# Sixteen block sums made ahead of the second attention's token product, and the copies of the keys' products dealt out anew

## The chip, the cores and the metric

The kernel runs on one core of a Trainium2 chip. The core has a matrix engine (TensorE, "PE" in the profile), a vector engine (VectorE, "DVE"), a scalar engine (ScalarE, "ACT"), a general engine (GpSimd, "POOL") and a queue that issues the loads and stores (SyncE, "SP"). The metric is the device time of one execution in microseconds, the median of several. Three executions of the kernel before took 1470.37, 1470.67 and 1471.87 us.

## The reference

Four layers work on a sequence of 2048 tokens of width 1024: linear attention, a gated feed-forward layer, and both once more with the same weights. Each layer takes the normalised input and adds its result to the input. The linear attention is, cut to its core:

```python
q, k, v = split(layernorm(x) @ wqkv)          # 32 heads of width 32
phi = lambda t: where(t > 0, t + 1, exp(t)) + 1e-6
pq, pk = phi(q), phi(k)
kv  = einsum("bhsd,bhse->bhde", pk, v)        # sums over all tokens
z   = einsum("bhsd->bhd", pk)
out = x + (einsum(pq, kv) / (einsum(pq, z) + 1e-6)) @ wo
```

## The kernel before

The 2048 tokens are 16 tiles of 128; four tiles make a quarter. The kernel never forms `v`. It forms the **token product** M, the transposed normalised input times `pk` summed over all tokens, and multiplies that by the weights of `v` afterwards. The stage is the function `m_products`.

**Seven products instead of eight.** Many of the large products use Strassen's scheme in Winograd's form: a product of two-by-two blocks takes seven block products, for which sums and differences of blocks have to be made first on VectorE. In `m_products` the token axis is halved, so tile `i` (0 to 7) goes with tile `NS + i` (8 to 15), and the width is halved into columns 0 to 511 and 512 to 1023. For each `i` eight sums are made, four of the normalised input (`n1` to `n4`) and four of the keys (`k1` to `k4`), all through `op` (L514); together 64, each of 128 by 512 two-byte elements. They depend on one another: `n2` needs `n1`, and `n4` needs `n2`, the keys likewise. `n1`, `n2`, `k1` and `k2` write into the memory of `x[8+i]`, whose contents have by then been sent away to DRAM; the others overwrite halves of their own inputs.

**The order in `m_products`.** TensorE goes through seven products of 32 matmuls each, and after every eight matmuls calls `later.tick()`. `later` holds tasks by due tick. The 64 sums are handed out four to a tick, in the order (`n1`,`k1`), (`n2`,`k2`), (`n3`,`k3`), `n4`, `k4`:

```python
jobs = [(f, i) for fs in ((n1, k1), (n2, k2), (n3, k3), (n4,), (k4,))
        for i in range(NS) for f in fs]
for n, (f, i) in enumerate(jobs):
    later.at(1 + n // 4, lambda f=f, i=i: self.behind(last_k, f, (i,)))
```

so they take ticks 1 to 16. `behind` queues them after the last key's last instruction. The first two products need no sums; the third reads `n1` and `k1`, the fourth `n2` and `k2`, the fifth `n4`, the sixth `n3` and `k3`, the seventh `k4`. The third product's result is copied by ScalarE (`keep`), and after each quarter of the fourth product VectorE adds that copy to the fourth's result (`add`, L556); the fifth product accumulates onto these sums. Here VectorE and GpSimd run in the order written (`manual_schedule`); elsewhere the compiler's planner orders each engine's instructions by program order and its own estimate of when each can start.

**The denominators** run beside it, from tick 10 on: `z_mult` (GpSimd, L690) multiplies a query tile by the keys' sums, `z_sum` two ticks later (VectorE, L695 to L697) sums by head, adds the small constant and inverts, `z_scale` two ticks later (GpSimd, L702) scales the tile, and `q_turn` (SP, L711) transposes it by DMA. `z_chain` starts the next tile two or three ticks after the last. All use one buffer, `ksum`, so the product of a tile waits for the reduction of the tile before it.

**The second attention ahead of it** (`l == 2`). Eight units of the first quarter's keys are run (`first`, eight ticks). Then `todo`, a hand-made list of 24 units, alternates keys of the second quarter with the queries of quarters 0 and 1, which `blocks("q", 0)` makes by the seven-product scheme in four steps (`one` to `four`) for each of four token tiles `j`; one unit of the third quarter's queries is put in as well. The other seven of these follow, and `blocks("k", 2)` makes the keys of quarters 2 and 3, the tiles `j` in pairs. Each result goes through `phi`: ScalarE's relu (L407) and exp (L408), then VectorE's join (L411). In `one`, two PSUM results are copied: the first product's onto bank `Y`, and the fifth's (`v`) to SBUF. For queries ScalarE makes both; for keys VectorE copies `Y` for odd `j` and `v` for every `j` (L635), ScalarE the rest (L637). `v` has bank `kv0` for every `j` of the keys, so a `v` waits for the copy of the one before it. Each key tile is also added into `ksum` on GpSimd (L482).

**After `m_products`** come the third quarter's remaining queries and `fold_wo` (L726), which needs the output weights `o0`. Their load is issued on SP while the seventh product runs, in SP's order behind transposed query tiles.

Of the kernel before, what the change touches and what calls it, by code (L numbers as in the profile page):

```python
# [10 lines left out]
F32 = mybir.dt.float32  # L11
# [3 lines left out]
P = 128  # L15
NW = 512
HD = 32
QT = 4
# [74 lines left out]
class _Net:  # L93
# [345 lines left out]
    def layer_A(self, l, last_ln):  # L439
# [5 lines left out]
        kv = []  # L445
# [79 lines left out]
        def m_products(q_first):  # L525

            NS = self.NS
            copy = lambda out, src: nc.scalar.activation(out=out, in_=src, func=ACT.Copy)
            X = [self.ps.tile([P, NW], F32, tag="a", name=f"mx{j}") for j in range(QT)]
            Y = [self.ps3.tile([P, NW], F32, tag="b", name=f"my{j}") for j in range(2)]  # L530
            Y += [self.kvp.tile([P, NW], F32, tag=f"kv{j}", name=f"my{2 + j}") for j in range(2)]
            mt, V, M5 = [], [], []
            last_k = self.last_phi
            jobs = [(f, i) for fs in ((n1, k1), (n2, k2), (n3, k3), (n4,), (k4,))
                    for i in range(NS) for f in fs]
            for n, (f, i) in enumerate(jobs):
                later.at(1 + n // 4, lambda f=f, i=i: self.behind(last_k, f, (i,)))

            def product(A, B, banks, start, done):
                for j in range(QT):  # L540
                    for i in range(NS):
                        nc.tensor.matmul(banks[j], lhsT=A(i)[:, j * P:(j + 1) * P], rhs=B(i),  # L542
                                         start=start and i == 0, stop=i == NS - 1,
                                         skip_group_check=True)
                    done(j)
                    later.tick()

            def evict(banks, h, n):
                return lambda j: copy(half(mt[h][:, j, :], n), banks[j])

            def keep(j):
                M5.append(self.temp(name="m5"))
                copy(M5[j], V[j])

            def add(out, j):
                nc.vector.tensor_tensor(out=out, in0=Y[j], in1=M5[j], op=ALU.add)  # L556

            product(lambda i: half(xn(i), 0), lambda i: half(pk(i), 0), X, True,
                    lambda j: copy(Y[j], X[j]))
            mt += [self.slot(f"mt{l}_{h}", [P, 4, D]) for h in range(2)]  # L560
            product(lambda i: half(xn(NS + i), 0), lambda i: half(pk(NS + i), 0), X, False,
                    evict(X, 0, 0))
            z_row()
            later.at(2 if l else 6, lambda: z_chain(0))
            V += [self.ps.tile([P, NW], F32, tag="a", name=f"mv{j}") for j in range(QT)]
            product(lambda i: part(i, 0), lambda i: part(i, 2), V, True, keep)
            product(lambda i: part(i, 1), lambda i: part(i, 3), Y, False, lambda j: add(V[j], j))
            product(lambda i: f16(half(xn(NS + i), 0)), lambda i: half(pk(NS + i), 1), V, False,
                    evict(V, 0, 1))
            product(lambda i: f16(half(xn(i), 1)), lambda i: f16(half(pk(i), 1)), Y, False,  # L570
                    lambda j: add(half(mt[1][:, j, :], 1), j))
            kv.extend(self.ps.tile([P, NW], F32, tag="a", name=f"kv{l}_{i}") for i in range(H))

            def steps(h, b):
                for j in range(QT):
                    kv_half(h * QT + j, mt[h][:, j, :], b)

            def last(j):
                copy(half(mt[1][:, j, :], 0), Y[j])
                if j < 3:  # L580
                    steps(*((0, 1), (1, 1), (0, 0))[j])
                if j == 1:
                    ring.load_to(ring.index((l, "o0")) + 1)

            product(lambda i: half(xn(NS + i), 1), lambda i: f16(half(pk(NS + i), 0)), Y, False, last)
            q_first()
            later.tick()
            steps(1, 0)
            ring.load_to(ring.index((l, "o1")) + 1)
            finish_kv()  # L590
# [19 lines left out]
        def blocks(p, first):  # L610


            xa, xb = self.xnT[l, first], self.xnT[l, first + 1]
            s1, s2, s3, s4 = self.xs[l, first // 2]
            r0, r1, t0, t1 = (ring.get((l, n)) for n in (f"{p}0", f"{p}1", f"t{p}0", f"t{p}1"))
            t0, t1 = (t[:, :, :].bitcast(F16) for t in (t0, t1))
            A = {1: xa[:, 0:4], 2: xa[:, 4:8], 3: s4, 4: xb[:, 4:8], 5: s1, 6: s2, 7: s3}
            B = {1: r0[:, 0:4], 2: r0[:, 4:8], 3: r1[:, 4:8], 4: t1[:, 0:4], 5: t0[:, 0:4],
                 6: t1[:, 4:8], 7: t0[:, 4:8]}
            if p == "q":  # L620
                for sc in range(first, first + 2):
                    a = self.slot(f"pq{l}_{sc}", [P, QT, D])
                    for i in range(QT):
                        pq_of[sc, i] = a[:, i, :]

            def put(src, q, j, n):
                t = (first + q) * QT + j
                cols = slice(n * NW, (n + 1) * NW)
                self.phi(src, (pq_of[first + q, j] if p == "q" else self.pk_home(l, t))[:, cols])
                if p == "k":  # L630
                    later.at(1, lambda: k_sum(t, cols))

            def copy(out, src, vector):
                if vector:
                    nc.vector.tensor_copy(out=out, in_=src)  # L635
                else:
                    nc.scalar.activation(out=out, in_=src, func=ACT.Copy)  # L637

            def steps(j):
                S = {}  # L640

                def mm(m, bank, start=False):
                    for k in range(4):
                        nc.tensor.matmul(by_row(bank), lhsT=A[m][:, k, j * P:(j + 1) * P],  # L644
                                         rhs=B[m][:, k, :].rearrange("p (b i d) -> p i b d", i=R, d=HD),
                                         start=start and k == 0, stop=k == 3, skip_group_check=True)

                def one():
                    S["X"] = self.ps.tile([P, NW], F32, tag="a", name=f"qx{j}")
                    mm(1, S["X"], True)  # L650
                    if p == "k" and j == 2:
                        S["Y"] = self.kvp.tile([P, NW], F32, tag="kv1", name=f"qy{j}")
                    else:
                        S["Y"] = self.ps3.tile([P, NW], F32, tag="b", name=f"qy{j}")
                    copy(S["Y"], S["X"], p == "k" and j % 2)
                    v = self.kvp.tile([P, NW], F32, tag=f"kv{j % 2 if p == 'q' else 0}", name=f"qv{j}")
                    mm(5, v, True)
                    S["V"] = self.temp(name="qm5")
                    copy(S["V"], v, p == "k")

                def two():
                    mm(2, S["X"])
                    put(S["X"], 0, j, 0)
                    mm(6, S["Y"])
                    S["Z"] = self.ps.tile([P, NW], F32, tag="a", name=f"qz{j}")
                    nc.vector.tensor_tensor(out=S["Z"], in0=S["Y"], in1=S["V"], op=ALU.add)

                def three():
                    mm(7, S["Y"])
                    nc.vector.tensor_tensor(out=S["V"], in0=S["Y"], in1=S["V"], op=ALU.add)  # L670
                    put(S["V"], 1, j, 1)
                    mm(3, S["Z"])
                    put(S["Z"], 0, j, 1)

                def four():
                    mm(4, S["Y"])
                    put(S["Y"], 1, j, 0)

                return one, two, three, four

            return [steps(j) for j in range(QT)]
# [144 lines left out]
        def run(*lists):  # L826

            n = max(len(u) for u in lists)
            for i in range(n):
                for u in lists:  # L830
                    if i < len(u):
                        u[i]()
                        later.tick()

        if l == 0:
            steps = self.head()
        else:
            ring.load_to(ring.index((l, "tq1")) + 1)
            for j in range(QT):
                later.at(1 + j, lambda j=j: self.sums_x(l, 0, j))  # L840
# [19 lines left out]
        else:  # L860
# [4 lines left out]
            for j in range(QT):  # L865
                todo += [next(k), Q[j][1], next(k), Q[j][2]] + ([Q[j + 1][0]] if j + 1 < QT else []) + [Q[j][3]]
            q2 = row_major(q_unit, 2)
            run(todo[:-1] + q2[:1] + todo[-1:])
            later.at(1, lambda: ring.load_to(ring.index((l, "tk1")) + 1))
            self.xs[l, 1] = [self.x[self.NS + i][:, :].bitcast(F16).rearrange("p (a n) -> p a n", n=NW)  # L870
# [433 lines left out]
```

## Time and profile before

| engine | busy of 1468.3 us | instructions |
|---|---|---|
| TensorE matmul | 1456.5 (99%) | 6927 |
| VectorE | 872.9 (59%) | 1546 |
| ScalarE | 577.5 (39%) | 1037 |
| GpSimd | 287.1 (20%) | 190 |

The second attention spans about 736 to 945 us of the profile. Its stages can be told apart by the lines of TensorE's instructions: L465 and L644 are projections, L542 the token product, L498 the product with the weights of `v`, L726 the fold, L738 the output.

| stage | from, us | to, us |
|---|---|---|
| first quarter's keys | 736.4 | 750.0 |
| `todo` and the third quarter's queries | 750.0 | 801.8 |
| keys of quarters 2 and 3 | 801.8 | 827.3 |
| token product | 827.3 | 885.8 |
| remaining queries, fold, output | 885.8 | 944.9 |

In the views, a row of the waits gives who waited for whom, the total in us, how often, and the longest. A row of the chain gives the start, the length, and the engine, tile and line. A row of the timeline also names output, inputs and shape, and in brackets the idle time before it.

### The profile page before, as it was taken

The numbers are of one execution on the slowest core, as the hardware profiler recorded it, in microseconds if no ns is written. First come the engines' busy times: TensorE is split into PE (matmuls) and PEld (weight loads), VectorE is DVE, ScalarE is ACT, GpSimd is POOL, SyncE is SP. The second block draws the span as 40 slices with busy tenths as digits, with TensorE's granted clock in tenths as the row PEclk, the third lists the DMA queues.
The fourth block names the chain that finished last, engine by engine and source line by source line (L and its number), as shares of the span: only waits on it lengthen the run. The fifth ranks groups of instructions, "written<-read, shape, count | busy, mean of one in ns | idle before, by whom it ended". The sixth has DMA issues, their size and how long they took to land.

```text
span 1468.3 us, 18717 instructions
## 1 busy us (share of the span) xinstructions
PE 1456.5 (99%) x6927; PEld 660.3 (45%) x6927; DVE 872.9 (59%) x1546; ACT 577.5 (39%) x1037; POOL 287.1 (20%) x190
## 2 busy tenths in 40 slices
PE   9999999999999999999999989999999999999999
PEld 4444444444444444444444434444444444444444
DVE  7978698666684654455476886766445434433632
ACT  6772574333340333340078616633333203333200
POOL 1354851011100011110031577410110001111000
PEclk9999999999999999999999999999999999999999
DMA  9940787564559996445933119965444687444461
GB/s 283 236 155 10 184 217 205 186 219 165 202 169 259 342 300 216 143 143 187 297 97 87 58 29 259 274 228 186 144 143 151 180 260 249 147 147 148 149 204 43
DMA packets 323883, 268.09 MB, mean 183 GB/s; under 512 B 106064, under 2 KB 295888, under 8 KB 321872
## 3 DMA queue, kind: packets, MB, share of 16 engines
q1 hardware_dynamic: 312784, 245.60, 56.7%
q10 hardware_dynamic: 11008, 21.30, 3.9%
q8 instruction: 54, 0.88, 0.2%
q14 instruction: 37, 0.30, 0.1%
HBM read 203.42 MB, written 38.80 MB: 165 GB/s over the span
## 4 chain that ended last, share of the span: by engine, by line
PE 93%; DVE 3%; DMA 1%; ACT 1%; POOL 1%; issue 0%; SPq 0%; DVEq 0%; ACTq 0%; POOLq 0%
PE ps L465 11%; PE dy L1150 10%; PE yu L1051 10%; PE yg L1051 10%; PE dx L1150 7%; PE dv L1150 7%; PE xg L1051 6%; PE xu L1051 6%; PE ps L738 4%; PE zg L1051 3%; PE zu L1051 3%; PE vu L1051 3%; PE vg L1051 3%; PE my L542 2%; PE mx L542 2%; PE qy L644 1%
## 5 line engine op out<-in xcount | busy, mean ns | idle before, releaser
L1051 PEld LDWEIGHTS <-w 128*128 128x128 f16 (+1 forms) x3136 | 306.7, 98 | 371.9 <-issue 2.5
L1104 POOL TENSOR_TENSOR h<-m5u,m5g 128x512 f16<-128x512 f32 x56 | 72.0, 1285 | 810.6 <-DVE m5u L1100 760.2
L465 PE MATMUL ps<-w,xnT 128*128 128x512 bf16 x768 | 170.1, 379 | 0.5 <-DMA w<-in_A_wqkv_dram 0.3
L1150 PEld LDWEIGHTS <-h 128*128 128x128 f16 x1120 | 109.6, 98 | 132.2
L1087 DVE TENSOR_TENSOR zg<-yg,m5g 128x512 f32<-128x512 f32 x56 | 39.2, 699 | 188.5 <-PE yg L1051 185.1
L1051 PE MATMUL yg<-s,w 128*128 128x512 f16 x448 | 115.0, 379 | 0.1
L465 PEld LDWEIGHTS <-xnT 128*128 128x128 bf16 x768 | 74.3, 98 | 90.5 <-issue 1.7
L1051 PE MATMUL yu<-s,w 128*128 128x512 f16 x448 | 115.0, 379 | 0.0
L1051 PE MATMUL xg<-xnT,w 128*128 128x512 f16 x448 | 115.0, 379 | 0.0
L1051 PE MATMUL xu<-xnT,w 128*128 128x512 f16 x448 | 115.0, 379 | 0.0
L1059 ACT ACTIVATE m5g<-m5g 128x512 f32<-128x512 f32 x56 | 35.2, 629 | 174.8 <-DVE m5g L1100 174.8
L1150 PE MATMUL dy<-w,h 128*128 128x512 f16 x448 | 98.0, 379 | 0.0
L1150 PE MATMUL dx<-w,h 128*128 128x512 bf16 x448 | 97.3, 379 | 0.0
L408 ACT ACTIVATE e<-e,eps 128x512 f32<-128x512 f32 x128 | 91.0, 720 | 3.3
L690 POOL TENSOR_TENSOR kvc<-pq,kvc 128x1024 f32<-128x1024 bf16 x32 | 78.5, 2452 | 60.1 <-DVE den L695 39.7
L738 PE MATMUL ps<-T,pqT 128*128 128x512 bf16 x384 | 83.6, 379 | 0.0
L1068 ACT ACTIVATE m5g<-vg 128x512 f32<-128x512 f32 x56 | 33.4, 597 | 110.9 <-PE vg L1051 85.2
L482 POOL TENSOR_TENSOR kvc<-kvc,slab 128x512 f32<-128x512 f32 x46 | 56.8, 1240 | 79.9 <-DVE slab L411 79.3
L1062 DVE TENSOR_TENSOR h<-yu,r 128x512 f16<-128x512 f32 x56 | 38.7, 691 | 56.0 <-PE yu L1051 56.0
L407 ACT ACTIVATE e<-ps 128x512 f32<-128x512 f32 x96 | 56.6, 590 | 34.1 <-PE ps L465 33.6
L1100 DVE TENSOR_TENSOR m5u<-yu,m5u 128x512 f32<-128x512 f32 x56 | 38.7, 691 | 49.4 <-PE yu L1051 48.4
L1150 PEld LDWEIGHTS <-e 128*128 128x128 f16 x448 | 43.8, 98 | 52.8
(191 smaller groups left out, 2108.4 us busy)
## 6 DMA issues: line engine op xcount, KB each, us to landing
w<-in_B_W_gate_dram SPq DMA_DIRECT2D x56, 512.0 KB, 5.7
w<-in_B_W_up_dram SPq DMA_DIRECT2D x56, 512.0 KB, 5.3
w<-td SPq DMA_DIRECT2D x32, 896.0 KB, 4.7
w<-in_B_W_down_dram SPq DMA_DIRECT2D x24, 896.0 KB, 5.3
w<-tg SPq DMA_DIRECT2D x42, 512.0 KB, 6.9
w<-tu SPq DMA_DIRECT2D x42, 512.0 KB, 6.5
w<-in_A_wqkv_dram SPq DMA_DIRECT2D x9, 1024.0 KB, 7.5
away<-x SPq DMA_DIRECT2D x16, 512.0 KB, 4.5
```

Of the source, the lines that this page charges most:

```text
L407: nc.scalar.activation(out=e, in_=ps, func=ACT.Relu, scale=-1.0)
L408: nc.scalar.activation(out=e, in_=e, func=ACT.Exp, scale=-1.0, bias=self.eps6[:, 0:1])
L465: nc.tensor.matmul(by_row(ps), lhsT=self.xnT[l, l_q][:, kt, j * P:(j + 1) * P], rhs=w[:, kt, :].rearrange("p (b i d) -> p i b d", i=R, d=H ...
L482: nc.gpsimd.tensor_tensor(out=ksum[:, cols], in0=ksum[:, cols], in1=pk, op=ALU.add)
L542: nc.tensor.matmul(banks[j], lhsT=A(i)[:, j * P:(j + 1) * P], rhs=B(i), start=start and i == 0, stop=i == NS - 1, skip_group_check=True)
L690: nc.gpsimd.tensor_tensor(out=prod, in0=pq_of[sc, j], in1=zrow, op=ALU.mult)
L738: nc.tensor.matmul(ps, lhsT=pqT[sc][:, g, j * P:(j + 1) * P], rhs=T[g // 4][:, g % 4, n2 * NW:(n2 + 1) * NW], start=(g == 0), stop=(g == G ...
L1051: nc.tensor.matmul(ps, lhsT=W[w][m][:, k, :], rhs=A[m][:, k, :], start=start and k == 0, stop=k == 3, skip_group_check=True)
L1062: self.last_put = nc.vector.tensor_tensor(out=h[:, b, :], in0=ps, in1=R.pop(b), op=ALU.mult)
L1087: self.last_z = nc.vector.tensor_tensor(out=Z[w], in0=Y[w], in1=V[w], op=ALU.add)
L1104: nc.gpsimd.tensor_tensor(out=h[:, 3, :], in0=V["u"], in1=V["g"], op=ALU.mult)
L1150: nc.tensor.matmul(banks[j], lhsT=A(k)[:, j * P:(j + 1) * P], rhs=w[:, i, :], start=start and k == 0, stop=k == self.U - 1, skip_group_che ...
```

## The change

Two things are changed, both in the second attention alone.

**The sums.** For `i` = 4 to 7, the sums `n1`, `n2`, `n3` and `k1` are made while the queries run, four to a batch, at ticks 16, 19, 22 and 25 after the first eight units; each batch is queued behind the join that was the last one then. `m_products` leaves these 16 out of its list and hands out the other 48, still four to a tick. The aim is to take work from VectorE in the token product and give it to a stretch where VectorE has room.

**The copies.** For the keys' seven-product tiles, the copies of `Y` for `j` = 0 and of `v` for `j` = 0 are ScalarE's, all others VectorE's. `Y` of tile 2 thus moves from ScalarE to VectorE, and `v` of tile 0 from VectorE to ScalarE. `v` of tile 1 goes to bank `kv1`, so that it no longer waits for the copy of tile 0's.

```diff
+            made = made_early
             jobs = [(f, i) for fs in ((n1, k1), (n2, k2), (n3, k3), (n4,), (k4,))
-                    for i in range(NS) for f in fs]
+                    for i in range(NS) for f in fs if (f, i) not in made]
...
-                    copy(S["Y"], S["X"], p == "k" and j % 2)
-                    v = self.kvp.tile([P, NW], F32, tag=f"kv{j % 2 if p == 'q' else 0}", name=f"qv{j}")
+                    copy(S["Y"], S["X"], p == "k" and j)
+                    v = self.kvp.tile([P, NW], F32, tag=f"kv{j % 2 if p == 'q' or j < 2 else 0}", name=f"qv{j}")
                     mm(5, v, True)
                     S["V"] = self.temp(name="qm5")
-                    copy(S["V"], v, p == "k")
+                    copy(S["V"], v, p == "k" and j)
...
+        made_early = set()
+
+        def make_early(ticks, *fs):
+
+            for tick, i in ticks:
+                for f in fs:
+                    made_early.add((f, i))
+                later.at(tick, lambda i=i: [self.behind(self.last_phi, f, (i,)) for f in fs])
...
             q2 = row_major(q_unit, 2)
+            make_early([(16 + 3 * j, QT + j) for j in range(QT)], n1, n2, n3, k1)
             run(todo[:-1] + q2[:1] + todo[-1:])
```

## The prediction

> **What bounds the kernel now.** I first read the busy times and the slices: TensorE is busy for 99% of the span at nearly full clock, so a change to VectorE's work pays only where TensorE waits. The waits of TensorE over the second attention (745 to 945 us) show where that is:
>
> ```profile
> PE mv L542 <- DVE slab L514: 2.7, 3, 1.7
> PE mv L542 <- DVE mv L556: 1.8, 1, 1.8
> PE qv L644 <- DVE qm L635: 0.9, 1, 0.9
> PE fold L726 <- DMA w<-in_A_wo_dram: 0.8, 1, 0.8
> ```
>
> The columns are total, times, longest. Four waits, 6.2 us. The upper two lie in the fifth block product (bank `mv`): for sums `n4` (tile `slab`, L514) and for the additions of L556. The third lies in the keys, for a copy that the change deals out anew; the fourth is the fold's wait for `o0`. The query stretch shows no wait of TensorE.
>
> Waits alone understate the fifth product. The windows have, after the times: length, then busy time of PE, PEld, DVE, ACT, POOL, then clock, DMA share, GB/s:
>
> ```profile
> 749.90:801.80 51.90, 51.90 (x243) 23.50 (x240) 32.33 (x56) 44.05 (x75) 12.72 (x11) 1.00 0.24 62
> 855.40:869.30 13.90, 9.46 (x33) 3.55 (x33) 13.83 (x23) 1.79 (x3) 6.47 (x4) 0.88 0.20 40
> 859.60:863.40 3.80, 3.76 (x10) 1.41 (x11) 3.73 (x8) 0.60 (x1) 1.60 (x1) 0.55 0.20 39
> ```
>
> The fifth product takes 13.9 us. Its 32 matmuls need 32 x 0.216 = 6.9 us (64 of the same shape take 13.83 us in the chain, 0.216 each). So 7.0 us are lost, with VectorE busy 13.8 of 13.9. The third row shows that part of it isn't idleness: for 3.8 us the clock was 0.55.
>
> Why VectorE is late is in the chain:
>
> ```profile
> 843.03 9.18 POOL kvc L690
> ...
> 852.23 1.23 DVE den L695
> ...
> 853.98 0.66 DVE mv L556
> 854.64 4.01 DVE slab L514 x4
> 858.65 0.61 DVE mv L556
> 859.26 1.33 DVE slab L514 x4
> 860.59 1.14 DVE den L695
> ...
> 862.24 0.67 DVE mv L556
> 862.91 4.01 DVE slab L514 x4
> 866.92 0.62 DVE mv L556
> ```
>
> This is VectorE's written order: ticks 1 to 12 hold 48 sums, then comes the first denominator, then the four additions with the last 16 sums (`n4`, `k4`) between them. VectorE ends its 48 sums at about 850.1, then stands 2.0 us, because the denominator waits for GpSimd's product:
>
> ```profile
> 843.03 9.17 POOL L690 TENSOR_TENSOR kvc<-pq,kvc 128x1024 f32<-128x1024 bf16 x1 [8.19 <-ACT kvc L492]
> 853.53 2.12 POOL L690 TENSOR_TENSOR kvc<-pq,kvc 128x1024 f32<-128x1024 bf16 x1 [1.33 <-DVE den L695]
> ```
>
> The same instruction takes 9.17 us while sums stream and 2.12 us otherwise. Conversely, four sums begun after GpSimd's took 4.01 us, against 1.33 us undisturbed.
>
> [...]
>
> **The change part by part.**
>
> *Token product.* The list shrinks from 64 to 48: `n1`,`k1` 8, `n2`,`k2` 12, `n3`,`k3` 12, `n4` 8, `k4` 8. At four a tick they end with tick 12, where in order of issue they still precede the first denominator. So the stream before it stays at 48 sums, ending at about 850.1: I give the first three 0.82 + 1.30 + 1.29 us as now (they collide with GpSimd's key sums), the other 45 0.336 each. GpSimd's first product stays locked out until then, and the first denominator still ends at 853.97. But no sums are left between the additions. The first is then done at 854.64, before the fifth product starts at 855.4. The second follows at 855.3 (needed 857.1). Then comes the second denominator: GpSimd's product ends at 855.65, so it runs to 857.45, and the third addition ends at 858.1 (needed 858.8), the fourth at 858.7 (needed 860.6). `n4` runs at about 844 to 847; it overwrites what the second product reads until 841.1, so it needn't wait. All 7.0 us go, slow clock included, the tightest margin being 0.7 us. **-7.0.**
>
> *Does the denominator chain hold the stages after it?* It now runs at GpSimd's pace, one product and one scaling in 2.07 + 1.88 = 3.95 us. The sixth scaling, behind which SP issues `o0`, ended at 885.93; it should end at 857.7 + 5 x 3.95 = 877.5. So it comes forward by more than TensorE does.
>
> *Fold.* `o0` was issued at 887.29, 1.4 us after that scaling, and landed 5.5 us later; now it lands at about 884.4. TensorE reaches the fold at 892.0 - 7.0 = 885.0. `finish_kv`'s scaling on VectorE (L594, now ending at 892.1) moves with TensorE and costs some 0.2. I take 0.6 of the 0.8 us. **-0.6**, between -0.8 and 0.
>
> *Keys.* Moving tile 0's `v` copy to ScalarE and tile 1's `v` to `kv1` removes a wait of 0.1 us at 805.84. ScalarE stood idle for 1.62 us there, which hides its new copy. For tile 3, `v` still waits in `kv0` for tile 2's copy, and VectorE now has tile 2's `Y` copy to make beside it. It was held by a join to 816.5, made another to 817.1 and the copy to 817.7; with one more 0.6 us copy in front, the 0.9 us wait becomes 1.5. **+0.5**, between -1.0 (planner puts the copies early) and +1.0.
>
> *Early sums.* They add 16 x 0.336 = 5.4 us to VectorE in a stretch where it is idle 51.9 - 32.3 = 19.6 us. By the units, the batches come due when TensorE is at about 776, 780, 786 and 790. Their inputs are there: the last tile's normalisation ends at 767.6, the second quarter's key tiles at about 759, 769, 778 and 788, and the stores from `x[12]` to `x[15]` are issued by 737.7. So nothing behind a batch waits for data. Behind it queue the joins, which release PSUM banks, and the additions L666 and L670, whose results or banks TensorE needs 1.7 to 1.9 us later (784.97 to 786.69 and 787.50 to 789.28). A batch is 1.34 us; if each of its sums met a key sum on GpSimd, it would be 4 x 1.30 = 5.2 us, but GpSimd is busy only 12.7 of 51.9 us. **+0.3**, between 0 and 1.5.
>
> Sum: -7.0 - 0.6 + 0.5 + 0.3 = -6.8, from 1470.67 to **1463.8 us**. TensorE has almost no idle time after the fold, and the later loads are issued as it frees buffers, so the gain should last to the end. The first attention's list has nothing early and is unchanged.
>
> **The rivals.** *Partial*: a wait takes the place of the one removed. Margins in the fifth product are 0.7 us; if the second denominator comes 2 us late, the third addition makes TensorE wait and its clock may drop again, and the query batches cost their upper 1.5. Half of the 7.0 stays: 1467.2. For it speaks the denominators' place ahead of the third addition; against it, GpSimd's 2.12 us is steady once sums no longer stream. *Nothing*: the 16 sums give TensorE 7 us of waits elsewhere, about 4 a batch: 1470.7. Against it, idle time of 19.6 us. *Slower*: batches keep meeting GpSimd's key sums, each 5.2 us long, and the joins behind hold PSUM banks. After 1.8 us of slack each would cost 3.4, together 13.6, less 7: 1477. For it speak the first three stretched sums at 831.6, against it GpSimd's 25% share.
>
> **How the numbers follow.** Forecast 0.75, partial 0.15, nothing 0.05, slower 0.05. The forecast's bounds run from -7.0 - 0.8 - 1.0 = -8.8 to -7.0 + 1.0 + 1.5 = -4.5, so 1461.9 to 1466.2; with most of the partial case the range is 1461.8 to 1467.4. A difference of 0.2% is 2.9 us: faster than 1467.7 are the forecast and the partial case, 0.90; same 0.05; slower 0.05.
>
> **What would show it.** Right: the fifth product in about 7 us at full clock; no L514 between the L556 additions; the first L690 still about 9 us; 16 L514 between 770 and 795 at about 0.4 us, with TensorE still unwaiting there; the key wait on L635 about 1.5 us. Wrong: waits of TensorE on joins or L666 in the queries, L556 behind L695 in the fifth product's waits, or a longer wait for `o0`.

## The result and the profile after

The changed kernel took 1461.71 us (median of four executions, 1461.67 to 1462.35) against 1470.52 us before: 8.8 us less, a ratio of 0.9939 with a 95% interval of 0.9922 to 0.9956. The direction and most of the working were right; the time fell 0.1 us below the range's lower end of 1461.8, and 2.1 us below the predicted 1463.8.

TensorE's waits in the second attention, in the kernel after (who waited for whom: total us, times, longest; the added lines shift the line numbers after them by up to eleven):

```profile
PE qx L645 <- DVE qy L636: 0.3, 1, 0.3
PE qv L645 <- DVE qm L636: 0.2, 1, 0.2
PE fold L727 <- DVE kvc L595: 0.2, 1, 0.2
```

Both waits of the fifth product and the fold's wait for `o0` are gone. The windows of the query stretch and of the fifth product (length, busy PE, PEld, DVE, ACT, POOL, clock, DMA share, GB/s):

```profile
749.42:801.22 51.80, 51.80 (x242) 23.48 (x241) 38.33 (x70) 43.60 (x75) 12.83 (x11) 1.00 0.22 62
854.33:861.24 6.91, 6.91 (x34) 3.14 (x33) 5.57 (x8) 1.79 (x3) 6.91 (x5) 1.00 0.36 42
```

The fifth product takes 6.91 us instead of 13.9, at a granted clock of 1.00 instead of 0.88. The query stretch is as long as before, although VectorE is busy there for 38.3 instead of 32.3 us. The chain, where VectorE and GpSimd stood between 843 and 867 us, is now TensorE alone:

```profile
840.68 6.91 PE mv L543 x32
847.59 6.91 PE my L543 x32
854.49 6.91 PE mv L543 x32
861.40 8.63 PE my L543 x40
```

GpSimd's first two denominator products, and VectorE around them, in the timeline:

```profile
842.00 9.17 POOL L691 TENSOR_TENSOR kvc<-pq,kvc 128x1024 f32<-128x1024 bf16 x1 [8.19 <-ACT kvc L492]
852.50 2.12 POOL L691 TENSOR_TENSOR kvc<-pq,kvc 128x1024 f32<-128x1024 bf16 x1 [1.33 <-DVE den L696]
```

```profile
843.74 5.45 DVE L514 TENSOR_TENSOR slab<-slab,x 128x512 f16<-128x512 bf16 x16
851.21 1.22 DVE L696 TENSOR_REDUCE den<-kvc 128x32 f32<-128x1024 f32 x1 [2.02 <-POOL kvc L691]
...
852.95 1.27 DVE L557 TENSOR_TENSOR mv<-my,m 128x512 f32<-128x512 f32 x2
854.66 1.22 DVE L696 TENSOR_REDUCE den<-kvc 128x32 f32<-128x1024 f32 x1 [0.45 <-POOL kvc L691]
...
856.84 1.27 DVE L557 TENSOR_TENSOR mv<-my,m 128x512 f32<-128x512 f32 x2
```

The first product takes 9.17 us as before, the second 2.12. But `n4` and `k4` now run in one stream of 16 ahead of the denominator (5.45 us, 0.34 each), and the additions (now L557) follow in pairs.

Lengths by stage, read from the starts of TensorE's first instruction of each in the timelines, in us:

| stage | before | after | difference |
|---|---|---|---|
| start of the profile to the first query product | 750.00 | 749.42 | -0.58 |
| queries, to the keys of quarters 2 and 3 | 51.80 | 51.80 | 0.00 |
| these keys, to the token product | 25.50 | 25.06 | -0.44 |
| token product, to the first fold | 65.53 | 57.84 | -7.69 |
| first fold to the last matmul | 571.78 | 572.05 | +0.27 |
| sum | 1464.61 | 1456.17 | -8.44 |

### The profile page after: what moved, and what is told of

Read it like the earlier page. It is cut to its first block, busy times and chain, and to the rows that moved or that the text cites. A ratio compares the mean times of both kernels' runs of the same rounds, so it can differ in the third digit from the quotient of the medians.

```text
span 1459.8 us, 18714 instructions
## 1 busy us (share of the span) xinstructions
PE 1453.1 (100%) x6927; PEld 659.9 (45%) x6927; DVE 869.3 (60%) x1546; ACT 576.5 (39%) x1037; POOL 286.7 (20%) x190
## 3 DMA queue, kind: packets, MB, share of 16 engines
q1 hardware_dynamic: 312784, 245.60, 57.6%
## 4 chain that ended last, share of the span: by engine, by line
PE 96%; DVE 2%; ACT 1%; issue 0%; DMA 0%; DVEq 0%; ACTq 0%
PE ps L465 11%; PE dy L1161 10%; PE yu L1062 10%; PE yg L1062 10%; PE dv L1161 7%; PE dx L1161 7%; PE xu L1062 6%; PE xg L1062 6%; PE ps L739 4%; PE zg L1062 3%; PE zu L1062 3%; PE vu L1062 3%; PE vg L1062 3%; PE my L543 3%; PE mx L543 2%; PE mv L543 2%
## 5 line engine op out<-in xcount | busy, mean ns | idle before, releaser
L691 POOL TENSOR_TENSOR kvc<-pq,kvc 128x1024 f32<-128x1024 bf16 x32 | 78.5, 2454 | 53.1 <-DVE den L696 32.8
```

The source lines that it names most:

```text
L691: nc.gpsimd.tensor_tensor(out=prod, in0=pq_of[sc, j], in1=zrow, op=ALU.mult)
```

## The experiments

Two theories were set against each other for the large part. **Order**: the additions and the last sums (`n4`), which the fifth product reads, were late because the denominator, with a GpSimd product that took 9.17 us beside the stream of sums, stood ahead of them, and because these sums stood between the additions. **Amount**: VectorE had more work than the stage had time for. For the small part the question was what the copies do.

**The sums without the copies, and the copies without the sums.** The first keeps the three lines on copies as they were, the second makes only these changes:

```diff
-copy(S["Y"], S["X"], p == "k" and j % 2)
+copy(S["Y"], S["X"], p == "k" and j)
...
-copy(S["V"], v, p == "k")
+copy(S["V"], v, p == "k" and j)
```

(and the bank of `v`).

> The sixteen sums early, the keys' copies dealt out as before. Theory A (each part has its own gain): the fifth product loses none of its 7.0 us and the fold 0.4 of its 0.8, and the keys keep the waits of before, so about 1463.0 us, some 1 us above the changed kernel, with the wait on L635 near 0.9 us. Rival B (the copies do nothing, all came from the sums): the same as the changed kernel within 0.3 us, 1461.7. Rival C (the early sums push VectorE's work into the start of the keys, so that the old copies get worse): over 1464.

> The copies dealt out anew, all 64 sums in the token product. Theory A: the keys gain what the two traces show, 0.27 us at the first tile pair and 0.26 at the second, so 0.3 to 0.8 us faster than before, with the fifth product still taking 13.9 us. Rival B, the prediction's step: 0.5 us slower than before.

Sums alone: 1462.86 us (ratio 0.9947, 0.9933 to 0.9960). From the token product to the fold it takes 57.85 us, as the changed kernel does. The keys take 25.86 us, 0.36 more than before and 0.80 more than with the new copies, because of this wait:

```profile
PE qv L645 <- DVE qm L636: 1.5, 1, 1.5
```

So theory A holds for the time, but not for the wait, for which it had 0.9 us: the early sums do make the old copies a little worse, by which path was not tested. Copies alone: 1470.15 against 1471.32 us, ratio 0.9995 (0.9987 to 1.0004), too little for times to tell; by stage, the keys take 25.05 us, 0.45 less than before, and the token product up to the fold 65.64 us. The keys' stage refutes the prediction's step, 0.5 us slower.

**All 64 sums ahead of the first denominator.**

```diff
-                later.at(1 + n // 4, lambda f=f, i=i: self.behind(last_k, f, (i,)))
+                later.at(1 + n // 6, lambda f=f, i=i: self.behind(last_k, f, (i,)))
```

> The kernel before, but its 64 sums are handed out six to a tick, so that all stand before the first denominator and none between the additions of L556. Theory A (GpSimd's product is locked out as long as sums stream, and the first addition stands behind it): the stream ends at about 855.5, the denominator at 859.3, the first addition at 860.0, where the fifth product was due at 855.4; TensorE loses 4.6 us and perhaps 1.7 more at the slow clock, so 0.6 to 2.4 us faster than before, 1468 to 1470. Rival B (what costs is only that sums stand between the additions): all 7 us gained, 1463.

1469.54 us against 1471.32 (ratio 0.9989, 0.9981 to 0.9997): 1.8 us faster, as theory A has it. By stage, the fifth product still loses 6.4 us instead of 7.0, and the fold no longer waits for `o0`. (The first attention runs through the same line; there the edit changed nothing, 57.6 us from the token product to the fold in both kernels.) GpSimd's first product in this kernel's timeline, and TensorE's one wait in the token product:

```profile
842.48 14.53 POOL L690 TENSOR_TENSOR kvc<-pq,kvc 128x1024 f32<-128x1024 bf16 x1 [8.19 <-ACT kvc L492]
```

```profile
PE mv L542 <- DVE mv L556: 4.5, 1, 4.5
```

With 16 more sums in the stream, 16 x 0.336 = 5.4 us, the product takes 14.53 instead of 9.17 us, 5.36 more. It ended 2.0 us after the last of these sums (857.01 and 855.03 us), as in the kernel before (852.20 and 850.21): it lasted as long as they streamed. Clearing the sums from between the additions brings only 0.6 of the fifth product's 7.0 us while the denominator stands ahead.

**The denominators four ticks later**, and nothing else: no early sums, no new copies.

```diff
-            later.at(2 if l else 6, lambda: z_chain(0))
+            later.at(6, lambda: z_chain(0))
```

> The kernel before, but the chain of denominators starts four ticks later; all 64 sums stay in the token product, with the last 16 between the additions. Theory A (the additions were late because the denominator and its locked-out GpSimd product stand ahead of them): the additions follow the fourth product directly, the fifth loses at most 0.5 us, the load of o0 comes behind four transposes and in time, so 6.5 to 7.5 us faster than before, 1463 to 1464. Rival B (VectorE has too much work in this stage, 64 sums don't fit whatever their order): less than 3 us faster. Rival C (the later denominators hold up the fold's weights): the fifth product is whole but the fold waits 4 us or more, 1466 to 1468.

1463.44 us against 1471.32 (ratio 0.9951, 0.9939 to 0.9964), 7.9 us faster. From the token product to the fold it takes 58.51 us, 7.0 less than before. TensorE's waits in this kernel are two:

```profile
PE qv L644 <- DVE qm L635: 0.9, 1, 0.9
PE fold L726 <- DMA w<-in_A_wo_dram: 0.8, 1, 0.8
```

VectorE during the fourth and fifth products, from its timeline, and GpSimd's first product:

```profile
851.86 0.70 DVE L556 TENSOR_TENSOR mv<-my,m 128x512 f32<-128x512 f32 x1 [0.24 <-PE my L542]
852.47 2.42 DVE L514 TENSOR_TENSOR slab<-slab,x 128x512 f16<-128x512 bf16 x4
854.82 0.69 DVE L556 TENSOR_TENSOR mv<-my,m 128x512 f32<-128x512 f32 x1
855.42 1.41 DVE L514 TENSOR_TENSOR slab<-slab,x 128x512 f16<-128x512 bf16 x4
...
860.63 1.20 DVE L695 TENSOR_REDUCE den<-kvc 128x32 f32<-128x1024 f32 x1
```

```profile
844.45 9.16 POOL L690 TENSOR_TENSOR kvc<-pq,kvc 128x1024 f32<-128x1024 bf16 x1 [8.20 <-ACT kvc L492]
```

All 64 sums are there, 12 of them between the additions and 4 behind the last, and the fifth product loses nothing. So order is the cause, not amount. Two parts of the order go together here and were not separated: the denominator no longer stands ahead, and most of the sums between the additions no longer meet a GpSimd instruction (1.41 us for four, against 4.01 before). The kernel before held similar evidence: its first attention already starts the denominators four ticks later (the `6` in the edited line), with all 64 sums in the token product, and there TensorE takes 57.6 us from the token product to the fold and waits for none of them. The prediction had named the place in the queue; it had not seen that the early sums are only one way to mend it. The load of `o0` came behind four transposes instead of six, so that the later denominators made the fold wait no longer than before, 0.8 us.

**The copy of tile 2's `Y` back on ScalarE; `v` of tile 1 back in `kv0`.** Each undoes one of the three copy edits.

```diff
-copy(S["Y"], S["X"], p == "k" and j)
+copy(S["Y"], S["X"], p == "k" and j % 2)
```

> The changed kernel, but the copy of Y of tile 2 is ScalarE's again, as before the change. Theory A (VectorE's copy of Y is what lets TensorE fill the wait for v of tile 3 with tile 2's second product, which overwrites what the copy reads): ScalarE has relus and exps queued until about 817, so that product waits over 1 us on ScalarE and the kernel is 0.4 to 1.0 us slower than the changed one, 1462.1 to 1462.7. Rival B, the prediction's step (each more copy on VectorE ahead of v of tile 2 costs 0.6 us): 0.3 to 0.6 us faster, 1461.1 to 1461.4.

```diff
-v = self.kvp.tile([P, NW], F32, tag=f"kv{j % 2 if p == 'q' or j < 2 else 0}", name=f"qv{j}")
+v = self.kvp.tile([P, NW], F32, tag=f"kv{j % 2 if p == 'q' else 0}", name=f"qv{j}")
```

> The changed kernel, but v of tile 1 is in kv0 again. Theory A (ScalarE's early copy of v of tile 0 frees the bank in time, the second bank does little): within 0.3 us of the changed kernel. Rival B (the bank is what freed the order): 0.5 us or more slower, with a wait for v of tile 1 or 3.

The first took 1462.52 us, with the keys at 25.24 us, 0.18 above the changed kernel. Theory A's time came out, but not by its wait: TensorE doesn't wait for ScalarE, but for `v` of tile 3 again:

```profile
PE qv L645 <- DVE qm L636: 0.9, 1, 0.9
```

TensorE's order is the planner's here, and it moved. In the changed kernel tile 2's second product is put ahead of `v` of tile 3 and fills most of the wait. TensorE's timeline of the changed kernel, then of this one, whose order and wait at this place are those of the kernel before:

```profile
815.03 1.03 PE L645 MATMUL qx<-w,xnT 128*128 128x512 bf16 x4
816.38 1.02 PE L645 MATMUL qx<-w,xnT 128*128 128x512 bf16 x4 [0.32 <-DVE qy L636]
817.57 1.02 PE L645 MATMUL qv<-w,x 128*128 128x512 f16 x4 [0.16 <-DVE qm L636]
```

```profile
815.41 1.03 PE L645 MATMUL qx<-w,xnT 128*128 128x512 bf16 x4
817.35 1.02 PE L645 MATMUL qv<-w,x 128*128 128x512 f16 x4 [0.91 <-DVE qm L636]
```

The one bank took 1461.92 us with the keys at 25.06 us and the same two waits: as theory A has it, the second bank does nothing measurable.

**All early sums in one burst.**

```diff
-            make_early([(16 + 3 * j, QT + j) for j in range(QT)], n1, n2, n3, k1)
+            make_early([(25, QT + j) for j in range(QT)], n1, n2, n3, k1)
```

> The changed kernel, but all four batches of early sums come due at once at the end of the hand-made list instead of over nine ticks. Theory A (VectorE has the room where the batches were put, but not at the start of the keys): some 4 us of sums are pushed against the keys' own sums and copies, which TensorE then waits for: 1.5 to 4 us slower than the changed kernel, 1463.2 to 1465.7. Rival B (there is slack anywhere ahead of the token product): within 0.5 us of it.

1463.52 us; the keys take 26.52 us, 1.46 more than in the changed kernel, at the lower end of theory A. TensorE's waits grow to this:

```profile
PE qx L645 <- DVE qy L636: 1.9, 3, 1.0
```

The sums themselves are free where the change put them and not at the end of the list, where VectorE's 16 sums for the keys follow.

**Tile 2 of the keys sooner.** The changed kernel with the steps of the keys in another order:

```diff
-            run([K[j + i][n] for j in (0, 2) for n in range(4) for i in range(2)])
+            order = [(0, 0), (1, 0), (0, 1), (1, 1), (0, 2), (1, 2), (2, 0), (0, 3), (1, 3), (3, 0),
+                     (2, 1), (3, 1), (2, 2), (3, 2), (2, 3), (3, 3)]
+            run([K[j][n] for j, n in order])
```

> The changed kernel, but the first step of tile 2 of the keys stands ahead of the last steps of tiles 0 and 1, and that of tile 3 behind them, so that tile 2's copies have 1.7 us more. Theory A (the 0.9 us that the keys still lose are waits for these two copies): 0.5 to 0.9 us faster than the changed kernel, 1460.8 to 1461.2. Rival B (the earlier copies push the joins of tiles 0 and 1 back, and banks come free later): same or slower.

> The changed kernel once more, beside the next two on one chip. Theory A: the start of the kernel, which the change doesn't touch, differs from execution to execution by some tenths of a us up to 2 us, so the median lies within 1461.5 to 1462.5, and the profile's first query product of the second attention starts anywhere from 749.4 to 751.4 us, with 51.8 us to the keys and 25.06 from there to the token product whatever the start. Rival B: the start belongs to the changed kernel, 749.42 again within 0.1 us.

> The changed kernel with tile 2's first step sooner, once more and beside the changed kernel. Theory A: no wait is left in the keys, 24.17 us, and the time is 0.6 to 1.0 us under that of the changed kernel. Rival B: the 0.7 us between them in different jobs was the start, and the two are within 0.3 us.

It took 1461.02 us, and beside the changed kernel on one chip 1461.50 (1461.13 to 1461.68) against 1461.91 us (1461.85 to 1462.28). The keys take 24.2 us both times, 112 x 0.216, with no wait of TensorE; they took 25.05 in the changed kernel run again. So 0.9 us of waiting is gone, as theory A says. The times differ by 0.7 us in the first comparison, as expected, and by 0.4 in the second, less than expected. The start varies by as much: the first query product came at 749.42 and 750.04 us in the two profiles of the changed kernel, at 749.65 and 750.31 us in those of this one, and at 749.4 to 751.4 us over all profiles. The queries took 51.8 us in every one.

**No early sums, with the other remedies.** Denominators four ticks later as above, all 64 sums in the token product, the new copies, tile 2 sooner.

> No early sums: all 64 in the token product, with the denominators four ticks later, the copies as in the changed kernel, and tile 2's first step sooner. Theory A (the order at the denominator is the cause; early sums are one way to mend it): the fifth product takes 6.9 us, the keys 24.2, the fold waits 0.8 for its weights, so within 0.6 us of the same with early sums, 1461.0 to 1461.8. Rival B (without the early sums VectorE is short of time once the keys wait less): 1 us or more slower than with them.

1462.38 us against 1461.50 for the same with early sums, 0.9 us more: between the theories. The keys take 24.17 us and the fifth product loses nothing, so VectorE isn't short of time; what is left is mainly the fold:

```profile
PE fold L727 <- DMA w<-in_A_wo_dram: 1.5, 1, 1.5
```

In SP's own waits, the load itself stood 3.0 us for the query tiles' transposes to land:

```profile
SPq L40 <- DMA pqT<-pq: 3.0, 1, 3.0
```

It is issued at 879.10 us, against 877.69 in the first profile of the changed kernel with tile 2 sooner, where TensorE is at the same point (token product from 825.63 us in both). The early sums let the denominators start earlier, so that the transposes are out of the way of the load; in these two kernels that is what they add to the later denominators' remedy. The fastest version measured is the changed kernel with tile 2 sooner.

## Why the prediction was right, and where it failed

- **Token product: right.** Predicted -7.0 us; the fifth product shrank from 13.90 to 6.91 us. The pieces came as worked out: the first L691 at 9.17 us, the additions in pairs behind the denominators, GpSimd's steps at about 3.95 us apart. The experiments with six sums a tick and with later denominators show the cause. One reading of the prediction was inexact: of the last 16 sums, 12 stood between the additions and 4 behind them.
- **Fold: right in size, incomplete.** Predicted -0.6; from the token product to the fold the difference is -7.69, so -0.70 beyond the fifth product's 6.99. The leftover 0.2 us is on VectorE's scaling (L595), as predicted. But 0.27 us came back at the fourth fold, which was not in the sum. In the timelines the third fold's copies on ScalarE end at 896.15, and the fourth fold has a gap up to 896.19; in the kernel before TensorE came to it behind those copies anyway. The code gives the fold's fourth matmul the bank that the last of these copies reads, and the 0.27 us stand in every profile whose fold doesn't wait for `o0` and in none whose fold does. That it waits for this bank fits all that, but was not tested by an edit.

```profile
894.11 2.04 ACT L733 ACTIVATE T<-fold 128x512 bf16<-128x512 f32 x4
895.89 0.73 PE L727 MATMUL fold<-w,kvc 32*32 32x512 bf16 x16
```

- **Keys: the step that failed.** "With one more 0.6 us copy in front, the 0.9 us wait becomes 1.5": +0.5 in the sum, measured -0.44. The copy of `v` did come 0.6 us later after tile 2's own matmuls (2.67 us after those of `v` began, against 2.07, and 2.07 again with the copy of `Y` back on ScalarE). But the step took TensorE's order as fixed, and the planner moved 0.86 us of tile 2's work into the wait. So the extra copy on VectorE gained 0.18 us, the difference from the kernel with that copy on ScalarE, where the prediction had it cost 0.6. The removed first wait was worth 0.26 us instead of 0.1; together that is the -0.44. The term's range allowed -1.0, but for another reason (earlier copies).
- **Early sums: right, a little too dear.** Predicted +0.3, measured 0.00. Two of the 16 met a key sum on GpSimd and took 1.38 us, as in this batch of the timeline, shown with the key sum; TensorE waited for none of it.

```profile
788.81 0.42 DVE L514 TENSOR_TENSOR x<-x,slab 128x512 f16<-128x512 bf16 x1
789.14 1.38 DVE L514 TENSOR_TENSOR x<-x 128x512 f16<-128x512 bf16 x1
790.45 0.41 DVE L514 TENSOR_TENSOR x<-x,x 128x512 f16<-128x512 f16 x1
790.79 0.41 DVE L514 TENSOR_TENSOR x<-x 128x512 f16<-128x512 bf16 x1
```

```profile
789.04 1.20 POOL L482 TENSOR_TENSOR kvc<-kvc,x 128x512 f32<-128x512 f32 x1 [3.18 <-DVE x L411]
```

- **The range.** The stages that the change touches sum to -0.44 - 7.69 + 0.27 = -7.9, within the forecast's bounds of -8.8 to -4.5. With the keys as measured, the prediction's own sum would have been -7.7 us, 1462.9. Another -0.58 is the start of the kernel, where the time varied from profile to profile: it arises before the first attention's token product (at 105.06 and 104.49 us), and from there to the first query product both kernels take 644.9 us. The spans differ by 8.5 us and the medians by 8.8. The kernel before itself varied: beside the first experiments its 25 executions fell into two groups, 11 at 1469.9 to 1470.5 and 14 at 1471.1 to 1472.0; why was not tested. The three times of before already spread by 1.5 us, and the range left no room for that.

The partial rival and the two without gain are refuted by the stages: the third addition made nobody wait, and the query stretch didn't lengthen.

## What to carry to other kernels

When an engine is late whose instructions run in the order written, look at what stands ahead of the late instruction before counting its work. VectorE ran so here: in the kernel before, the first addition began at 853.97 us, behind the denominator and 3.76 us after the last of the 48 sums; four ticks' delay of one chain won 7.0 of the 7.7 us that moving a quarter of the sums won between the token product and the fold. In code that a planner orders, don't cost a delayed copy by the wait alone, but ask what independent work of the waiting engine can be put ahead of it. And widen a narrow range by the spread of the unchanged stretches, most of all the start.

## What the runs showed of the hardware beyond the expected

The denominators' first GpSimd product (L690), begun during a stream of VectorE sums without gaps, took 9.17 us with the stream of before and 14.53 us with 16 sums more. Both times it ended 2.0 us after the last sum, close to the 2.12 us that it takes without sums beside it, as if it had got no turn until then; the sums kept 0.336 us each. It needn't be the end of all sums: with later denominators the stream paused for 0.24 us at 851.6 us ahead of an addition, and the product ended 2.0 us later, at 853.6. The addition beside it kept its 0.70 us, while the four sums behind took 2.42 instead of 1.41.

Not every GpSimd instruction was held up like that. The key sum at 789.04 us began while a sum of a batch ran, and took 1.20 us (1.16 without sums beside it); it was the next sum, begun 0.1 us behind it, that took longer, 1.38 us instead of 0.41, and ended 0.28 us after it. In the kernel before, the first two of the four sums that took 4.01 us each ended 0.28 us after a GpSimd instruction, the product (855.65) and the scaling (857.70), and the last two came 0.34 us apart. So the scaling, too, got in between two sums: it took 2.08 us, against 1.91 without sums beside it. With the first product it was the other way: 21 sums that began after it ended before it. What decides this, the runs don't show.

After a gap of 4.7 us in the experiment with six sums a tick, TensorE's first three matmuls came 0.216 us apart and the next eight 0.43; gap and slow matmuls together cost 6.4 us. In the kernel before, matmuls came 0.43 us apart from 860.0 to 863.0 us, where the granted clock was 0.50, after five gaps since 855.4 us that add up to 3.4 us, the longest of 1.8. Whether the gaps bring this on, and for how long, was not tested.
